# Projection weights in one transfer per contraction tile, a gate column transposed by a matmul, and whole-tile x copies, in a gated mix of linear-memory attention and a gated feed-forward

## The chip, the cores and the metric

One core of a Trainium2 chip runs the kernel. The metric is device microseconds from launch to end; the median over several runs is given, and a profile of one execution shows what the engines did. Engines are named as the profile names them: PE (TensorE matmuls), PEld (its weight loads), DVE (VectorE), ACT (ScalarE), POOL (GpSimd), SP (SyncE, which here only issues DMA transfers). "SPq" and "ACTq" are DMA issues by SP and ACT.

## The reference

All inputs are bfloat16; x is 2048 tokens by 512 features. Two branches are computed from the same x and mixed by a gate of one number per token.

```python
x = A_x
g = sigmoid((x * gate_w).sum(-1, keepdims=True))
a = A_ref(x, wq, wk, wv, wo, beta)   # attention in 4 segments of 512 tokens, 32 heads of 16
b = B_ref(x, W_gate, W_up, W_down)   # (relu(x @ W_gate) * (x @ W_up)) @ W_down, inner size 1792
return g * a + (1 - g) * b
# inside A_ref, per segment s:
#   p = softmax(qs @ ks.T * 0.25 + causal mask); a_dot = p @ vs
#   a_mem = phi(qs) @ M / (phi(qs) @ z + 1e-6);  o = sigmoid(beta) * a_mem + (1 - sigmoid(beta)) * a_dot
#   M += phi(ks).T @ vs;  z += phi(ks).sum()      (phi(t) = t + 1 for t > 0, else exp(t))
# the segments' o are joined and multiplied by wo
```

## The kernel before

The work is cut into four segments of 512 tokens. For each segment the program builds lists of operations: the q, k and v projections (`proj`), causal attention (`att`), the update of the memory matrix (`mu`), the memory's numerator and denominator (`nd`), the feed-forward (`ffn`) and the output product (`outp`). 512 features are four contraction tiles of 128 (`KT = 4`, index `kt`). x is needed transposed, features on partitions, in the tile `xT`.

The order of instructions on each engine is not written by hand. `Sched` is a greedy list scheduler that runs while the kernel is built: each operation names what it reads and writes (strings such as `wq0` or `xT0_1a`), its engine and an estimated duration; queues carry priorities, and the scheduler repeatedly places the operation that its own clock says is ready first. It keeps its own estimate of when a transfer lands: bytes are added up over all transfers at 310 bytes per ns, plus 1.8 us for those issued early and 3.2 us for the others. What it emits is one fixed program per engine with semaphore waits where an operation depends on another engine or a transfer. Each engine runs its program in order, so an instruction whose wait is not met holds all behind it on that engine. Transfers share 16 semaphores in turn; the seventeenth transfer waits for an earlier one that used the same semaphore.

PSUM is used as four banks `psL` (the attention logits, and at the start the transposes of x) and four banks `psA` handed out to accumulations as they come (`Epoch`). If two engines read one bank the scheduler orders them.

The start goes as follows. SP and ACT each issue two of the four loads of segment 0's x (128 KB each, into `hT0` to `hT3`, L416). Then the three 512 x 512 projection weights follow, each in two transfers (L418 to L423): wq as contraction tiles 0 to 2 on SP (384 KB) and tile 3 on ACT; wk and wv as tiles 0 to 1 on ACT and 2 to 3 on SP. After them SP issues beta, the first halves of the feed-forward weights `wg` and `wu` (896 KB each, L431 and L432), the four transposing loads of segment 1's x (L436), the second halves of `wg` and `wu`, `wo` and `wd`. ACT also issues the gate weights as one column (L444): the 512 numbers are put as four columns over 128 partitions, so neighbouring elements of memory go to different partitions.

```python
lact.append(dma("act", ld_gw, 60000, writes=["gwc"], name="ldgw"))
lact[-1].after = 6500.0
```

The second line holds this issue back until 6.5 us of the scheduler's clock. Meanwhile PE runs six warm-up matmuls on zeros (L491), transposes segment 0's x by matmuls with an identity into the four `psL` banks, one bank for each 128 tokens (L499), and runs four more warm-up matmuls, which write the first of these banks again. Each bank is copied to `xT` in two halves: contraction tiles 0 and 1 by DVE (L506), 2 and 3 by ACT (L508). The q projection of segment 0 reads all of these copies; each of its accumulations is two operations of two matmuls, over tiles 0 and 1 and over 2 and 3 (L575), and each waits for the transfers that hold its tiles. The k and v projections (L575 and L573) and everything else follow. The gate of segment 0 is 16 one-column matmuls of `xT` with `gwc` (L531), an exponential on ACT (L535) and small operations behind it; the gate of the other three segments is done later in the same way.

Of the kernel before, what the change touches and what calls it, by code (L numbers as in the profile page):

```python
# [10 lines left out]
BF16 = mybir.dt.bfloat16  # L11
# [329 lines left out]
def plan(S, D, F):  # L341
# [13 lines left out]
        ("rden", [128, 32], F32), ("rdg", [128, 32], F32), ("rdm", [128, 128], F32), ("pm8", [128, 8], F32), ("pm", [128, 2], F32), ("ident", [128, 128], BF16),  # L355
# [24 lines left out]
def program(sc, nc, T, PL, PA, A_x, A_wq, A_wk, A_wv, A_wo, A_beta, W_g, W_u, W_d, gate_w, out, NSEG, KT, NF, NT, EPS, SCALE):  # L380
# [11 lines left out]
    def dve(fn, occ, **k):  # L392
        return op("dve", fn, occ, **k)
# [13 lines left out]
    def xt(c):  # L407
        return [f"xT{c}_{kt}" for kt in range(KT)] if c else [f"xT0_{i}{h}" for i in range(4) for h in "ab"]
# [8 lines left out]
    halves = {}  # L417
    for nm, w, src, cut, engs in (("wq", V.wq, A_wq, 3, ("sp", "act")), ("wk", V.wk, A_wk, 2, ("act", "sp")), ("wv", V.wv, A_wv, 2, ("act", "sp"))):  # L418
        r = src.rearrange("(kt p) n -> p kt n", p=128)
        for h, (k0, k1) in enumerate(((0, cut), (cut, KT))):  # L420
            load(engs[h], [f"{nm}{h}"], w[:, k0:k1, :], r[:, k0:k1, :], (k1 - k0) << 17)
            for kt in range(k0, k1):
                halves[nm, kt] = f"{nm}{h}"  # L423
# [16 lines left out]
    gsrc = gate_w.rearrange("(kt p) -> p kt", p=128)  # L440

    def ld_gw(e):
        with nc.allow_non_contiguous_dma(reason="one column of gate weights"):
            return e.dma_start(V.gwc[:], gsrc)  # L444
    lact.append(dma("act", ld_gw, 60000, writes=["gwc"], name="ldgw"))
    lact[-1].after = 6500.0
# [49 lines left out]
    for i in range(4):  # L496
        def fx(e, i=i):
            for kt in range(KT):
                ins = e.matmul(PL[:, i, kt * 128:(kt + 1) * 128], lhsT=V.hT[:, i, kt * 128:(kt + 1) * 128], rhs=V.ident[:], start=True, stop=True)  # L499
            return ins  # L500
        xps.append(pe(fx, 430, reads=[f"hT{i}", "ident"], writes=[f"bankL{i}"], name=f"xt{i}"))
        for h in range(2):
            dst = V.xT[:, 2 * h:2 * h + 2, i * 128:(i + 1) * 128]
            srcp = PL[:, i, 256 * h:256 * h + 256].rearrange("q (k t) -> q k t", k=2)
            if h == 0:
                xcs.append(dve(lambda e, d=dst, s_=srcp: e.tensor_copy(d, s_), t_dve(256), reads=[f"bankL{i}"], writes=[f"xT0_{i}a"], name=f"xc{i}"))  # L506
            else:
                xcs.append(act(lambda e, d=dst, s_=srcp: e.activation(d, s_, ACT.Copy), t_act(256), reads=[f"bankL{i}"], writes=[f"xT0_{i}b"], name=f"xc{i}"))  # L508
# [13 lines left out]

    gexpT_r = {}
# [26 lines left out]
    sc.queue(2, gq["pe"][:1])  # L550
    sc.queue(4, gq["pe"][1:])
    sc.queue(1, gq["act"])
# [9 lines left out]
    def proj(s):  # L562
# [3 lines left out]
        def pj(w, col, name, wname, tokmajor=False):  # L566
            ep = Epoch("proj")

            for k0 in range(0, KT, 2):
                def fn(e, k0=k0):  # L570
                    for kt in (k0, k0 + 1):
                        if tokmajor:
                            ins = e.matmul(A(ep)[:, :], lhsT=V.xT[:, kt, tok + col * 128:tok + (col + 1) * 128], rhs=w[:, kt, :], start=(kt == 0), stop=(kt == KT - 1))  # L573
                        else:
                            ins = e.matmul(A(ep)[:, :], lhsT=w[:, kt, col * 128:(col + 1) * 128], rhs=V.xT[:, kt, tok:tok + 512], start=(kt == 0), stop=(kt == KT - 1))  # L575
                    return ins
                pes.append(pe(fn, mm(512, 2), reads=sorted({halves[wname, k0], halves[wname, k0 + 1]}) + xt(s), name=f"{name}{s}_{col}", ep=ep, role="w2" if k0 else "w"))
# [309 lines left out]
```

The softmax here doesn't subtract the row's maximum and nothing guards it: scores larger than these inputs give would overflow.

## Time and profile before

| | us |
|---|---|
| median of 5 runs | 276.65 |
| lowest and highest | 276.54, 278.15 |
| the profiled execution | 276.64 |
| its span, first to last instruction | 274.90 |
| PE busy | 264.6 (96% of the span) |
| DVE busy | 198.9 (72%) |
| ACT busy | 191.3 (70%) |
| POOL busy | 92.4 (34%) |
| first projection matmul | 7.38 |
| last matmul ends | 272.10 |

A line of the profile names the source line, the engine, the operation, what is written from what is read, the number of instructions, and in square brackets how long the engine had been idle before and what ended that. In a list in order of time the first number is the start in us from the beginning of the span and the second how long the group lasted. The granted TensorE clock was 0.999 of full speed throughout.

### The profile page before, as it was taken

To read this page: it belongs to the slowest core of one execution; us is meant where nothing else is said; L and a number is where in the kernel's file an instruction comes from. 1 tells how busy PE (TensorE), PEld (TensorE's weight loads), DVE (VectorE), ACT (ScalarE), POOL (GpSimd) and SP (SyncE) were. 2 spreads that over 40 slices of the span, in tenths; PEclk is the share of its full clock that TensorE was granted. 3 is DMA by queue.
4 is the path that set the end of the run, shared out by engine and by line. 5 is a ranking of instruction groups with operands and counts; after the bars stand their busy time and mean duration, and the time that the engine had idled before them with its cause. 6 is when DMAs were issued, how large, how long until landed. Compare 5 with 4: busy or idle time off the path is not lost.

```text
span 274.9 us, 5331 instructions
## 1 busy us (share of the span) xinstructions
PE 264.6 (96%) x2168; PEld 116.2 (42%) x2204; DVE 198.9 (72%) x391; ACT 191.3 (70%) x170; POOL 92.4 (34%) x152
## 2 busy tenths in 40 slices
PE   7999999999999999999999999999999999999995
PEld 3444344434444444444344343344434343444444
DVE  5598989899999999978789774378677055857200
ACT  3089997898697787786679777785767777763112
POOL 4013234334445452535233434332333333320000
PEclk9999999999999999999999999999999999999999
DMA  7999533000101223040012000000110100000011
GB/s 234 319 246 365 159 76 80 0 3 20 41 1 38 41 60 57 19 60 0 2 38 41 1 21 19 21 19 2 38 38 2 38 21 19 2 1 0 2 38 39
DMA packets 29384, 15.29 MB, mean 56 GB/s; under 512 B 20784, under 2 KB 29360, under 8 KB 29360
## 3 DMA queue, kind: packets, MB, share of 16 engines
q1 hardware_dynamic: 27856, 14.04, 20.3%
q10 hardware_dynamic: 1504, 0.92, 1.1%
q8 instruction: 17, 0.28, 0.4%
q14 instruction: 7, 0.06, 0.1%
HBM read 8.14 MB, written 2.10 MB: 37 GB/s over the span
## 4 chain that ended last, share of the span: by engine, by line
PE 89%; DVE 4%; ACT 2%; DMA 2%; issue 2%; SPq 0%
PE psA L740 35%; PE psA L779 17%; PE psL L670 9%; PE psA L575 9%; PE psA L695 7%; PE psA L772 5%; PE psA L573 5%; ACT E L675 2%; DMA wq<-in_A_wq_dram 2%; PE psA L645 1%; PE psA L616 1%; DVE hT L751 1%; DVE kp L591 1%; DVE qT L582 0%; DVE adT L707 0%
## 5 line engine op out<-in xcount | busy, mean ns | idle before, releaser
L675 ACT ACTIVATE E<-psL 128x2048 bf16<-128x2048 f32 x80 | 150.1, 1876 | 40.2 <-PE psL L670 39.7
L678 POOL TENSOR_SCALAR_AFFINE_SELECT E<-E 128x512 bf16<-128x512 bf16 x128 | 82.8, 664 | 147.9 <-ACT E L675 145.6
L740 PE MATMUL psA<-xT,wg 128*128 128x512 bf16 x215 | 57.6, 380 | 1.4 <-issue 1.3
L740 PE MATMUL psA<-xT,wu 128*128 128x512 bf16 x217 | 57.7, 380 | 0.8 <-issue 0.6
L779 PE MATMUL psA<-wd,hT 128*128 128x512 bf16 (+1 forms) x228 | 53.5, 367 | 1.1 <-issue 0.8
L751 DVE TENSOR_TENSOR hT<-psA,rl 128x512 bf16<-128x512 f32 x56 | 38.4, 686 | 14.1 <-PE psA L740 12.7
L700 DVE STREAM_TRANSPOSE Tn<-psA 128x512 f32<-128x512 f32 x32 | 21.5, 700 | 19.2 <-PE psA L695 19.1
L670 PE MATMUL psL<-qT,kp 32*128 32x384 bf16 (+3 forms) x512 | 31.7, 301 | 0.4 <-ACT E L675 0.3
L779 PEld LDWEIGHTS psA<-wd,hT 128*128 128x128 bf16 x238 | 21.4, 98 | 23.6 <-issue 3.9
L740 PEld LDWEIGHTS psA<-xT,wu 128*128 128x128 bf16 x224 | 20.5, 98 | 25.3 <-issue 2.0
L740 PEld LDWEIGHTS psA<-xT,wg 128*128 128x128 bf16 x224 | 20.1, 98 | 25.1 <-issue 3.5
L748 ACT ACTIVATE rl<-psA 128x512 bf16<-128x512 f32 x29 | 17.2, 597 | 13.9 <-PE psA L740 11.3
L670 PEld LDWEIGHTS psL<-qT,kp 32*128 32x128 bf16 x512 | 8.9, 92 | 33.1 <-ACT E L675 18.0
L749 DVE TENSOR_SCALAR rl<-psA 128x512 bf16<-128x512 f32 x27 | 18.5, 684 | 4.4 <-PE psA L740 3.7
L695 PE MATMUL psA<-E,vaug 128*17 128x256 bf16 (+3 forms) x512 | 21.1, 300 | 0.2 <-DVE kT L588 0.2
L575 PE MATMUL psA<-xT,wq 128*128 128x512 bf16 x60 | 16.1, 380 | 1.5 <-DMA wq<-in_A_wq_dram 1.0
L789 ACT ACTIVATE osb<-psA,omg 128x512 bf16<-128x512 f32 (+1 forms) x10 | 6.4, 644 | 15.6 <-PE psA L772 13.3
L575 PE MATMUL psA<-xT,wk 128*128 128x512 bf16 x62 | 16.4, 380 | 0.1
L772 PE MATMUL psA<-wo,oT 128*128 128x512 bf16 (+1 forms) x65 | 15.8, 366 | 0.4 <-issue 0.3
L573 PE MATMUL psA<-wv,xT 128*128 128x512 bf16 x63 | 15.3, 380 | 0.2 <-issue 0.2
L695 PEld LDWEIGHTS psA<-E,vaug 128*17 128x17 bf16 x512 | 10.5, 90 | 11.2 <-issue 3.8
L582 DVE CAST qT<-psA 128x512 bf16<-128x512 f32 x16 | 10.9, 684 | 3.5 <-PE psA L575 3.4
(68 smaller groups left out, 211.4 us busy)
## 6 DMA issues: line engine op xcount, KB each, us to landing
out_dram<-osb SPq DMA_DIRECT2D x15, 128.0 KB, 1.7
wg<-in_B_W_gate_dram SPq DMA_DIRECT2D x2, 896.0 KB, 7.7
wu<-in_B_W_up_dram SPq DMA_DIRECT2D x2, 896.0 KB, 10.1
wd<-in_B_W_down_dram SPq DMA_DIRECT2D x1, 1792.0 KB, 13.9
wo<-in_A_wo_dram SPq DMA_DIRECT2D x1, 512.0 KB, 9.4
wq<-in_A_wq_dram SPq DMA_DIRECT2D x1, 384.0 KB, 5.5
hT<-in_A_x_dram ACTq DMA_DIRECT2D x2, 128.0 KB, 3.1
hT<-in_A_x_dram SPq DMA_DIRECT2D x2, 128.0 KB, 2.9
```

Source lines behind the costliest of these rows:

```text
L573: ins = e.matmul(A(ep)[:, :], lhsT=V.xT[:, kt, tok + col * 128:tok + (col + 1) * 128], rhs=w[:, kt, :], start=(kt == 0), stop=(kt == KT - 1))
L575: ins = e.matmul(A(ep)[:, :], lhsT=w[:, kt, col * 128:(col + 1) * 128], rhs=V.xT[:, kt, tok:tok + 512], start=(kt == 0), stop=(kt == KT - 1))
L670: ins = q.matmul(PL[:, jj, o:o + w], lhsT=V.kp[32 * jj:32 * jj + 32, kslot(s, n), 128 * j:128 * j + 128], rhs=V.qT[32 * jj:32 * jj + 32, q ...
L675: acts.append(act(lambda a, e=e: a.activation(V.E[:, e, :, :], PL[:, :, :], ACT.Exp, scale=SCALE), t_act(2048), reads=[f"bankL{b}" for b i ...
L678: pools.append(pool(lambda g, ap=ap: g.affine_select(out=ap, in_=ap, compare_op=ALU.is_ge, fill=0.0, base=0, pattern=[[0, 4], [1, 128]], c ...
L695: ins = q.matmul(A(ep)[32 * jj:32 * jj + 17, c:512], lhsT=V.vaug[:, s % 2, j, 8 * G + 2 * jj + p, :], rhs=V.E[:, e, jj, o:o + w], start=(j ...
L700: ds.append(dve(lambda e, p=p, ep=eps[p]: e.transpose(V.Tn[:, p, :], A(ep)[:, :]), t_dve(512), writes=[f"Tn{p}"], name=f"tr{s}_{G}_{p}", e ...
L740: ins = e.matmul(A(ep)[:, :], lhsT=w[:, kt, f * 128:(f + 1) * 128], rhs=V.xT[:, kt, c * 512:(c + 1) * 512], start=(kt == 0), stop=(kt == K ...
L749: ("dve", lambda e, ep=eg, r=r: e.tensor_scalar(V.rl[:, r, :], A(ep)[:, :], 0.0, None, ALU.max), t_dve(512))],
L751: evs.append(dve(lambda e, ep=eu, r=r, hs=hs: e.tensor_tensor(V.hT[:, hs, :], A(ep)[:, :], V.rl[:, r, :], ALU.mult), t_dve(512), reads=[f" ...
L772: ins = e.matmul(A(ep)[:, 0:c1 - c0], lhsT=V.oT[:, o0 + G, i * 128:(i + 1) * 128], rhs=V.wo[:, G, c0:c1], start=st_ and G == 0, stop=sp_ a ...
L779: ins = e.matmul(A(ep)[:, 0:c1 - c0], lhsT=V.hT[:, slots[f], i * 128:(i + 1) * 128], rhs=V.wd[:, f, c0:c1], start=st_ and f == f0, stop=sp ...
```

## The change

Each of the three projection weights is loaded in four transfers, one for each contraction tile of 128 KB; wq's tiles 1 and 3 are issued by ACT, all other tiles by SP. A projection operation waits for the two tiles that it reads. The gate weights are loaded by SP as four rows of 128 numbers (`g4`, contiguous in memory), behind the first halves of `wg` and `wu`; a matmul with a 4 x 4 identity transposes them into a `psA` bank, and an ACT copy writes `gwc`. The x copies of segment 0 are one for each bank, all four contraction tiles at once, by DVE for banks 0 and 2 and by ACT for banks 1 and 3.

```diff
--- before.py
+++ after.py
@@ -352,7 +352,7 @@
         ("Mbd", [128, 4, 136], F32), ("Mbd16", [128, 4, 136], BF16), ("mumask", [128, 2, 136], BF16), ("mutmp", [128, 2, 136], F32),
         ("gwc", [128, KT], BF16), ("braw", [128, 32], BF16), ("eb", [128, 32], F32), ("romgh", [128, 32], F32), ("epsv", [128, 32], F32),
         ("gexp", [128, NT], F32), ("omg", [128, NT], F32), ("gexpT", [128, NT * 4], F32), ("c2g", [128, NT, 32], F32),
-        ("rden", [128, 32], F32), ("rdg", [128, 32], F32), ("rdm", [128, 128], F32), ("pm8", [128, 8], F32), ("pm", [128, 2], F32), ("ident", [128, 128], BF16),
+        ("rden", [128, 32], F32), ("rdg", [128, 32], F32), ("rdm", [128, 128], F32), ("pm8", [128, 8], F32), ("pm", [128, 2], F32), ("ident", [128, 128], BF16), ("g4", [4, 128], BF16),
     ]
 
 
@@ -405,7 +405,7 @@
         return PA[ep.bank]
 
     def xt(c):
-        return [f"xT{c}_{kt}" for kt in range(KT)] if c else [f"xT0_{i}{h}" for i in range(4) for h in "ab"]
+        return [f"xT{c}_{kt}" for kt in range(KT)] if c else [f"xT0_{i}" for i in range(4)]
 
     lact, lsp = [], []
 
@@ -414,13 +414,9 @@
     x0 = A_x[0, 0:512, :].rearrange("(i p) d -> p i d", p=128)
     for i, eng in enumerate(("sp", "act", "sp", "act")):
         load(eng, [f"hT{i}"], V.hT[:, i, :], x0[:, i, :], 1 << 17)
-    halves = {}
-    for nm, w, src, cut, engs in (("wq", V.wq, A_wq, 3, ("sp", "act")), ("wk", V.wk, A_wk, 2, ("act", "sp")), ("wv", V.wv, A_wv, 2, ("act", "sp"))):
-        r = src.rearrange("(kt p) n -> p kt n", p=128)
-        for h, (k0, k1) in enumerate(((0, cut), (cut, KT))):
-            load(engs[h], [f"{nm}{h}"], w[:, k0:k1, :], r[:, k0:k1, :], (k1 - k0) << 17)
-            for kt in range(k0, k1):
-                halves[nm, kt] = f"{nm}{h}"
+    for nm, w, src in (("wq", V.wq, A_wq), ("wk", V.wk, A_wk), ("wv", V.wv, A_wv)):
+        for kt in range(KT):
+            load("act" if nm == "wq" and kt % 2 else "sp", [f"{nm}{kt}"], w[:, kt, :], src[kt * 128:(kt + 1) * 128, :], 1 << 17)
     wgr = W_g.rearrange("(kt p) n -> p kt n", p=128)
     wur = W_u.rearrange("(kt p) n -> p kt n", p=128)
     half = (NF // 2) * 128
@@ -437,13 +433,7 @@
                            1 << 17, occ=1280.0, writes=[f"xT{c}_{kt}"], name=f"ldx{c}_{kt}"))
     load("sp", ["braw"], V.braw[:], A_beta.partition_broadcast(128), 8192)
     load_gu(0)
-    gsrc = gate_w.rearrange("(kt p) -> p kt", p=128)
-
-    def ld_gw(e):
-        with nc.allow_non_contiguous_dma(reason="one column of gate weights"):
-            return e.dma_start(V.gwc[:], gsrc)
-    lact.append(dma("act", ld_gw, 60000, writes=["gwc"], name="ldgw"))
-    lact[-1].after = 6500.0
+    load("sp", ["g4"], V.g4[:], gate_w.rearrange("(kt p) -> kt p", p=128), 1 << 12)
     load_x(1)
     load_gu(1)
     load("sp", ["wo"], V.wo[:], A_wo.rearrange("(g p) n -> p g n", p=128), 1 << 19)
@@ -499,13 +489,12 @@
                 ins = e.matmul(PL[:, i, kt * 128:(kt + 1) * 128], lhsT=V.hT[:, i, kt * 128:(kt + 1) * 128], rhs=V.ident[:], start=True, stop=True)
             return ins
         xps.append(pe(fx, 430, reads=[f"hT{i}", "ident"], writes=[f"bankL{i}"], name=f"xt{i}"))
-        for h in range(2):
-            dst = V.xT[:, 2 * h:2 * h + 2, i * 128:(i + 1) * 128]
-            srcp = PL[:, i, 256 * h:256 * h + 256].rearrange("q (k t) -> q k t", k=2)
-            if h == 0:
-                xcs.append(dve(lambda e, d=dst, s_=srcp: e.tensor_copy(d, s_), t_dve(256), reads=[f"bankL{i}"], writes=[f"xT0_{i}a"], name=f"xc{i}"))
-            else:
-                xcs.append(act(lambda e, d=dst, s_=srcp: e.activation(d, s_, ACT.Copy), t_act(256), reads=[f"bankL{i}"], writes=[f"xT0_{i}b"], name=f"xc{i}"))
+        dst = V.xT[:, :, i * 128:(i + 1) * 128]
+        srcp = PL[:, i, :].rearrange("q (k t) -> q k t", k=KT)
+        if i % 2 == 0:
+            xcs.append(dve(lambda e, d=dst, s_=srcp: e.tensor_copy(d, s_), t_dve(512), reads=[f"bankL{i}"], writes=[f"xT0_{i}"], name=f"xc{i}"))
+        else:
+            xcs.append(act(lambda e, d=dst, s_=srcp: e.activation(d, s_, ACT.Copy), t_act(512), reads=[f"bankL{i}"], writes=[f"xT0_{i}"], name=f"xc{i}"))
     xps.append(warm(4, 1, 0))
     sc.queue(0, xps)
     sc.queue(0, [t for t in xcs if t.eng == "dve"])
@@ -520,6 +509,9 @@
     sc.queue(0, [t for t in cst if t.eng == "act"])
     sc.queue(1, [t for t in cst if t.eng == "dve"])
 
+    ep_w = Epoch()
+    gw_pe = pe(lambda e: e.matmul(A(ep_w)[:, 0:KT], lhsT=V.g4[:, :], rhs=V.ident[0:KT, 0:KT], start=True, stop=True), 60, reads=["g4", "ident"], name="gwT", ep=ep_w, role="w")
+    gw_act = act(lambda e: e.activation(V.gwc[:], A(ep_w)[:, 0:KT], ACT.Copy), 180, writes=["gwc"], name="gwc", ep=ep_w, role="r")
     gexpT_r = {}
     gq = {"pe": [], "act": [], "dve": [], "flex": []}
     for part, (t0, t1) in enumerate(((0, 4), (4, NT))):
@@ -547,9 +539,9 @@
         if part:
             gq["dve"].append(dve(lambda e, t0=t0: e.tensor_tensor(V.c2g[:, t0:, :], V.eb[:, :].unsqueeze(1).to_broadcast([128, NT - t0, 32]), V.gexp[:, t0:].unsqueeze(2).to_broadcast([128, NT - t0, 32]), ALU.mult),
                                  t_dve((NT - t0) * 32), reads=["eb", f"gexp{part}"], writes=["c2g"], name="c2g"))
-    sc.queue(2, gq["pe"][:1])
+    sc.queue(2, [gw_pe] + gq["pe"][:1])
     sc.queue(4, gq["pe"][1:])
-    sc.queue(1, gq["act"])
+    sc.queue(1, [gw_act] + gq["act"])
     sc.queue(1, gq["dve"])
     sc.queue(2, gq["flex"])
 
@@ -574,7 +566,7 @@
                         else:
                             ins = e.matmul(A(ep)[:, :], lhsT=w[:, kt, col * 128:(col + 1) * 128], rhs=V.xT[:, kt, tok:tok + 512], start=(kt == 0), stop=(kt == KT - 1))
                     return ins
-                pes.append(pe(fn, mm(512, 2), reads=sorted({halves[wname, k0], halves[wname, k0 + 1]}) + xt(s), name=f"{name}{s}_{col}", ep=ep, role="w2" if k0 else "w"))
+                pes.append(pe(fn, mm(512, 2), reads=[f"{wname}{k0}", f"{wname}{k0 + 1}"] + xt(s), name=f"{name}{s}_{col}", ep=ep, role="w2" if k0 else "w"))
             return ep
         for G in range(4):
             ep = pj(V.wq, G, "q", "wq")
```

## The prediction

> **What bounds the kernel now.** I read first the page's busy shares, then the chain of waits, then its start instruction by instruction, because all that the change touches is issued in the first 20 us.
>
> ```profile
> PE 264.6 (96%) x2168; PEld 116.2 (42%) x2204; DVE 198.9 (72%) x391; ACT 191.3 (70%) x170; POOL 92.4 (34%) x152
> ...
> PE 89%; DVE 4%; ACT 2%; DMA 2%; issue 2%; SPq 0%
> ```
>
> ```profile
> 7.38:272.10 264.72, 259.63 (x2142) 113.77 (x2178) 195.24 (x381) 188.13 (x164) 88.98 (x137) 1.00 0.21 51
> ```
>
> The first two lines are the page's busy times and its chain by engine. Columns of the third (busy time by stretch): the stretch, its length, then busy time of PE, PEld, DVE, ACT, POOL. From the first projection matmul (7.38) to the last matmul (272.10) PE is busy 259.63 of 264.72 us; only 5.09 us are idle, in gaps of mostly 0.16 to 0.4 us. So whatever the change does to the first 20 us reaches the end only as a shift of the moment at which this dense block begins, as a new hole in it, or as a different number of gaps. The chain shows what sets its beginning:
>
> ```profile
> 1.73 5.52 DMA wq<-in_A_wq_dram
> 7.38 5.12 PE psA L575 x23
> ```
>
> ```profile
> 4.45 1.42 DVE L506 CAST xT<-psL 128x256 bf16<-128x256 f32 x4 [0.99 <-PE psL L499]
> 4.91 1.05 ACT L508 ACTIVATE xT<-psL 128x256 bf16<-128x256 f32 x3 [0.34 <-DVE xT L506]
> ...
> 4.96 10.86 SPq L436 DMA_TRANSPOSE xT<-in_A_x_dram  x4
> 5.59 0.38 ACTq L444 DMA_DIRECT2D gwc<-in_gate_w_dram  x1
> 6.02 0.38 ACT L508 ACTIVATE xT<-psL 128x256 bf16<-128x256 f32 x1
> ...
> 7.38 3.61 PE L575 MATMUL psA<-xT,wq 128*128 128x512 bf16 x16 [0.99 <-DMA wq<-in_A_wq_dram]
> ...
> 18.61 0.54 PE L531 MATMUL psA<-gwc,xT 128*128 128x1 bf16 x16
> ```
>
> The 384 KB transfer of wq, issued at 1.73, lands 5.52 us later, at 7.25; PE starts 0.14 later. The x copies are done at 6.02 + 0.38 = 6.40 and the warm-up matmuls at 6.39: these are second, 0.85 us ahead of the weights.
>
> **What the Trainium skill says.** "DMA: Bandwidth & Descriptors", section "Issuing engines are not separate DMA queues": transfers of all issuing engines run on the same 16 DMA engines and interleave; two issuers save only issue time. The trace agrees: between 3 and 8 us the core moves 343 to 380 GB/s with two queues filled, and from 11 to 14 us, with SP's alone left but for the gate column, 350 to 368. The same page, "Queues, rings and completion order": each DMA engine takes turns between the queues, in order within one. Here the ACT queue's third 128 KB (wq's last tile) landed at 1.73 + 4.5 = 6.2 and its fourth and fifth (half of wk) at 2.21 + 5.6 = 7.8: 0.8 us per 128 KB while SP's queue is full too. The same page, "Rules for kernel authors": a strided last dimension becomes one descriptor per element. The ACT queue's 1504 packets fit: 896 KB in rows of 1 KB are 896, which leaves room for 512 gate elements. "PSUM — Partial Sum Buffer", section "Terms": two engines must not read one bank at once. The ordering in the kernel respects it: ACT's first half copy waits 0.34 us for DVE's.
>
> **The change, part by part.**
>
> *wq by tiles.* Now both pairs of contraction tiles wait for the 384 KB transfer, since tiles 0 to 2 are one. After it, the first pair waits for tiles 0 and 1, third in their queues, the second for 2 and 3, fourth. By ACT's cadence above, tile 1 lands at 6.2 and tile 3 at 6.2 + 0.8 = 7.0; SP's tiles are earlier (its fifth 128 KB landed at 7.25, its seventh at 2.19 + 6.5 = 8.7, so 0.72 each, the fourth at 6.5). With the 0.14 us from landing to matmul the second pair starts at 7.14. Before, it started at 7.38 + 2 x 0.215 = 7.81 (16 matmuls in 3.61 us: 0.215 from start to start). **Gain 0.67 us.** Bounds: if landing no longer mattered the first pair would start at 6.34, second at 6.77, gain 1.04; if tile 3 lands as late as the 384 KB did, gain 0.42; if the four small transfers take longer still, nothing.
>
> *x copies.* PE makes the four transposed tiles 0.35 us apart (16 matmuls in 1.41), so they can be copied from 4.45, 4.80, 5.15, 5.50. A 512-wide PSUM copy costs 684 ns on DVE (row of L582) and 597 on ACT (row of L748): DVE 4.45 to 5.13 and 5.15 to 5.84, ACT 4.80 to 5.40 and 5.50 to 6.10. Done at 6.10 against 6.40. Priced at nothing: the landing of wq tile 1 at 6.2 hides it. The four warm-up matmuls wait for tile 0's copy, 5.13 against 5.29, and stay ahead of 6.3. Should the weights land at once, the copies would set the start, at 6.24.
>
> *ACT's queue* loses the two wk/wv halves (0.49 + 0.52 us) and the column's issue (0.38). Its table load, 1.28 us, moves from 3.29 to about 2.7; its first copy waits for PE in both versions. Nothing.
>
> *SP's queue* goes from 8 loads to 16 ahead of the transposes. Its cadence is 0.50 us (1.73 to 4.22 for five), so wk's last tile is issued at 4.2, wv's at 6.2, beta at 6.7, wg at 7.2 (before 3.75), wu at 7.7, the gate rows at 8.2, and the x transposes of segment 1 begin at 8.9 instead of 4.96. What waits behind each:
> - wk is needed when the 16 q matmuls end, 7.14 + 14 x 0.215 = 10.2. About 1.6 MB lie up to its last tile; at 350 GB/s from 2.3 us these have moved by 6.9, and some 1.3 us lie between the last byte and landing (the 384 KB: about 1.3 MB interleaved by 7.25, moved by 6.0). 8.2: covered by 2 us.
> - wv is needed at 14.0; it lands by 9.7. Covered. beta lands about 9.8, before 10.84: eb, which waited 4.5 us on ACT, and the romgh behind it lose their wait, off the path.
> - wg and wu: a 128 KB load is issued every 0.50 us and drained in 0.37, but SP's backlog built while ACT's queue shared the engines lasts until about 8.4, when wg's first bytes arrive (7.2 + 1.2). So the engines do not run dry; they land near 13.65 and 4.22 + 11.8 = 16.0 as before, against first uses near 19 and 20.4.
> - Segment 1's x, whose last transpose was issued at 14.24 and landed 3.8 us later, at 18.0. PE's first use stood at 19.0 and moves to 18.4. This is the thin cover, 0.4 us. The four issues took 10.86 us, where the undisturbed take 1.26 each; the first two lasted 3.18 and 4.43:
>
> ```profile
> 4.96 3.18 SPq L436 DMA_TRANSPOSE xT<-in_A_x_dram  x1
> ...
> 8.18 4.43 SPq L436 DMA_TRANSPOSE xT<-in_A_x_dram  x1
> ```
>
> They ended at 8.14 and 12.61, each 1.0 to 1.5 us ahead of the landing of wv (9.5) and of wg (3.75 + 9.9 = 13.65), as if each were let through when the load ahead had been drained. Then a start at 8.9 finds the first obstacle gone and ends no later than 15.8. I take a landing at 17 to 18; ends: 16.5, and 21.9 if the whole stretch moves by 3.9.
> - wg's and wu's second halves, wo and wd follow by at most 4 us: second halves are used from about 40 us and landed at 21.4 and 24.9. Covered.
>
> *Gate column.* Removed: 512 tiny transfers that landed at 5.59 + 8.6 = 14.2. Added: a 1 KB load behind wu (landing about 16), one 128x4 matmul and one ACT copy. The matmul costs like one of L531, 0.54/16 = 0.03 us, with a gap of 0.16 around it at most; the copy 0.17 (the gexp row, 128x4). The gate matmuls, at 18.61 before, then stand behind PE to ACT to PE, some 0.5 us if nothing fills it; the scheduler counts these latencies and has ffn work to put between. Waiting behind the gate matmuls on PE would be segment 1's projection. Cost 0 to 0.5, taken at 0.1.
>
> Sum: -0.67 + 0.10 = -0.57 us. The profiled execution took 276.64 us (span 274.90 and 1.74 around it), a hundredth below the median of 276.65. So 276.1.
>
> **The rivals.**
> 1. *No gain*: per-tile transfers share the same bandwidth and the last wq tile lands at 7.3 or later; then 276.6 to 277. For it: 128 KB pieces; against it: ACT's third piece landed at 6.2.
> 2. *The transposes come late* (slower). If the long issues are SP's own work and not back-pressure, all move by 3.9 us: landing 21.9, PE at 18.4 with segment 1's first q matmuls at its head and all else behind: 21.9 + 0.13 - 18.4 = 3.6 us of hole, net +3.0, 279.6. It decides from a landing at 18.3 on. Against it speak the two ends above and the 1.26 us of undisturbed issues.
> 3. *The order is made anew.* The list scheduler is greedy, and shifted estimates at the start can change which matmuls follow which over all 265 us. Gaps are 0.16 us each (L740 behind issue: 1.9 us in 12), and DVE is busy 38.15 of 40 us between 60 and 100, so a bad order costs. Twelve gaps more are +1.9, 278.0 in all; twelve fewer 274.2. Nothing in the profile says which.
>
> **How the numbers follow.** About 0.5% (1.4 us) is what a measurement of this kernel can tell from no change. Forecast (276.1, own range 275.4 to 276.7) 0.50; no gain 0.15; late transposes 0.13; worse order 0.14; better order or the full 1.04 us with luck 0.08. Faster by over 0.5%: 0.08 and a tenth of the forecast, 0.13. Slower: 0.14, most of 0.13 and a little of the forecast, 0.27. Between: 0.60. The range is 274.9 to 278.9: it takes in half of the order's swing upwards and half of the late transposes, and leaves some 0.07 below and 0.12 above.
>
> **What would show it.** First wq matmul near 6.35, the second pair behind a wait for wq to about 7.1; the 16 q matmuls ending near 10.3 (before 10.98); last x copy at 6.1; the transposes beginning at 8.9 and ended by 15.8; no hole of PE near 18.4; PE busy 259 to 260 us from the first projection matmul on. Wrong: a DMA wait for xT at 18 to 22 us, a start at 7.3 or later, or over 6 us idle in the dense block.

## The result and the profile after

The changed kernel takes 277.09 us (median of 43 runs) against 277.37 for the kernel before (80 runs): ratio 0.9989, 95% interval 0.9976 to 1.0002. A second set of runs gave 277.15 against 277.67, 0.998 [0.996, 1.0]. So it is the same, or faster by 0.1 to 0.2%; both intervals reach no change. Ratios are taken over fast executions alone (those within 1.5% of the fastest of their kernel), so they are not exactly the quotients of the medians. The profiled execution took 277.89 us with a span of 276.2, which is 0.8 us above its own median; the profiled execution of before, 276.64, lies 0.7 below its median of 80 runs. What is compared below has to allow for that.

The lines of the page that answer to those of before, busy times and chain by engine:

```profile
PE 264.6 (96%) x2169; PEld 115.8 (42%) x2205; DVE 198.6 (72%) x387; ACT 191.4 (69%) x171; POOL 92.3 (33%) x152
...
PE 84%; DVE 6%; DMA 3%; ACT 2%; issue 2%; SPq 2%; DVEq 0%
```

Busy time by stretch, from the first projection matmul to the last matmul (columns as before: stretch, length, busy time of PE and so on):

```profile
6.32:273.40 267.08, 259.87 (x2143) 113.75 (x2179) 194.99 (x379) 188.58 (x167) 88.89 (x137) 1.00 0.22 52
```

PE starts at 6.32 instead of 7.38, but the stretch is 267.1 us long instead of 264.7. A gain of 1.06 us at the start is lost, and 1.3 us besides. The start in order of time shows where. A hole is time in which PE stands idle; PEld lines are weight loads, one ahead of each matmul. First the kernel before, from its k projection on:

```profile
10.62 3.33 PEld L575 LDWEIGHTS psA<-xT,wk 128*128 128x128 bf16 x16
...
11.15 0.18 DVE L515 TENSOR_SCALAR romgh<-eb 128x32 f32<-128x32 f32 x1 [1.15 <-ACT eb L514]
11.24 0.68 DVE L582 CAST qT<-psA 128x512 bf16<-128x512 f32 x1
...
14.38 0.39 PE L670 MATMUL psL<-qT,kp 32*128 32x512 bf16 x4
```

Then the changed one:

```profile
4.27 1.29 DVE L495 CAST xT<-psL 128x512 bf16<-128x512 f32 x2 [0.81 <-PE psL L489]
4.50 1.09 ACT L497 ACTIVATE xT<-psL 128x512 bf16<-128x512 f32 x2 [0.54 <-PE psL L489]
...
6.32 3.81 PE L567 MATMUL psA<-xT,wq 128*128 128x512 bf16 x16 [0.26 <-DMA wq<-in_A_wq_dram]
6.52 0.43 SPq L413 DMA_DIRECT2D braw<-in_A_beta_dram  x1
...
8.50 9.61 SPq L432 DMA_TRANSPOSE xT<-in_A_x_dram  x4
9.75 3.33 PEld L567 LDWEIGHTS psA<-xT,wk 128*128 128x128 bf16 x16
...
13.63 0.23 ACT L503 ACTIVATE eb<-braw 128x32 f32<-128x32 bf16 x1 [8.04 <-DMA braw<-in_A_beta_dram]
13.89 0.18 DVE L504 TENSOR_SCALAR romgh<-eb 128x32 f32<-128x32 f32 x1 [3.04 <-ACT eb L503]
13.98 0.68 DVE L580 CAST kT<-psA 128x512 bf16<-128x512 f32 x1
...
15.67 0.39 PE L662 MATMUL psL<-qT,kp 32*128 32x512 bf16 x4 [2.09 <-DVE kp L583]
...
18.69 0.09 PEld L513 LDWEIGHTS psA<-ident,g 4*128 4x128 bf16 x1 [0.42 <-DMA g<-in_gate_w_dram]
...
19.48 0.54 PE L523 MATMUL psA<-gwc,xT 128*128 128x1 bf16 x16
```

Read it backwards from the hole. PE stands for 2.09 us because the masked k tile `kp` is not there. DVE has not made it because it stood still for 3.04 us: its next instruction in order is `romgh`, which needs beta's exponential. ACT could not make that because beta's 8 KB, issued by SP at 6.52, behind sixteen weight and x loads of which twelve are SP's, landed 7.09 us later, at 13.6. The four copies of k stood in DVE's program behind this one small operation; in the kernel before it was two copies of q, and PE did not yet need what waited for them.

The lengths of the parts show that this is nearly all. From the first weight load of k to the first attention matmul the changed kernel takes 5.92 us (9.75 to 15.67), the kernel before 3.76 (10.62 to 14.38): 2.16 us lost. From the start of q to the first weight load of k it takes 3.43 us instead of 3.24, because q's second pair waits for its tiles: 0.19 us. From the first attention matmul to the last matmul both take 257.7 us. Together 2.35 of the 2.38 us by which the stretch is longer. The weight load of the transposing matmul waited 0.42 us for the gate rows, but by these lengths that cost PE nothing here.

What fills the time in which beta is on its way is seen in the data rate (last column, GB/s; the one before it is the busy share of the DMA engines). First the kernel before, then the changed one:

```profile
9.00:10.00 1.00, 1.00 (x7) 0.42 (x5) 0.83 (x2) 0.00 (x0) 0.00 (x0) 1.00 0.84 283
```

```profile
9.00:10.00 1.00, 1.00 (x7) 0.43 (x5) 0.82 (x2) 0.00 (x0) 0.00 (x0) 1.00 0.55 104
```

The first pieces of beta move at 8.4 us, and in the microsecond shown the DMA engines move 104 GB/s where 350 are usual. What stands behind beta in SP's queue landed later too: the last of segment 1's x at 20.2 instead of 18.0. The trace counts the landing of a load in sixteen signals. For beta fifteen of them had come by 10.5 us; the sixteenth came at 13.6. So one late signal of a small load made the wait long.

### The profile page after: what moved, and what is told of

Its sections match the earlier page's. It is cut to its first block, busy times and chain, and to the rows that moved or that the text cites. A ratio compares the mean times of both kernels' runs of the same rounds, so it can differ in the third digit from the quotient of the medians.

```text
span 276.2 us, 5342 instructions
## 1 busy us (share of the span) xinstructions
PE 264.6 (96%) x2169; PEld 115.8 (42%) x2205; DVE 198.6 (72%) x387; ACT 191.4 (69%) x171; POOL 92.3 (33%) x152
## 3 DMA queue, kind: packets, MB, share of 16 engines
HBM read 8.14 MB, written 2.10 MB: 37 GB/s over the span
## 4 chain that ended last, share of the span: by engine, by line
PE 84%; DVE 6%; DMA 3%; ACT 2%; issue 2%; SPq 2%; DVEq 0%
PE psA L732 33%; PE psA L771 17%; PE psL L662 9%; PE psA L687 7%; PE psA L567 6%; PE psA L764 5%; PE psA L565 5%; DMA braw<-in_A_beta_dram 3%; ACT E L667 2%; SPq L413 2%; DVE hT L743 1%; PE psA L637 1%; PE psA L608 1%; DVE kT L580 1%; DVE kp L583 1%
## 5 line engine op out<-in xcount | busy, mean ns | idle before, releaser
L692 DVE STREAM_TRANSPOSE Tn<-psA 128x512 f32<-128x512 f32 x32 | 21.5, 700 | 19.2 <-PE psA L687 19.1
L741 DVE TENSOR_SCALAR rl<-psA 128x512 bf16<-128x512 f32 x27 | 18.5, 684 | 4.4 <-PE psA L732 3.7
L781 ACT ACTIVATE osb<-psA,omg 128x512 bf16<-128x512 f32 (+1 forms) x10 | 6.4, 644 | 15.6 <-PE psA L764 11.7
L764 PE MATMUL psA<-wo,oT 128*128 128x512 bf16 (+1 forms) x65 | 15.8, 366 | 0.4 <-issue 0.3
L687 PEld LDWEIGHTS psA<-E,vaug 128*17 128x17 bf16 x512 | 10.5, 90 | 11.2 <-issue 3.6
L583 DVE TENSOR_SCALAR kp<-kT,pm 128x512 bf16<-128x512 bf16 x32 | 12.4, 399 | 1.2 <-PE psL L662 0.8
```

Of the source, the lines that this page charges most:

```text
L687: ins = q.matmul(A(ep)[32 * jj:32 * jj + 17, c:512], lhsT=V.vaug[:, s % 2, j, 8 * G + 2 * jj + p, :], rhs=V.E[:, e, jj, o:o + w], start=(j ...
L692: ds.append(dve(lambda e, p=p, ep=eps[p]: e.transpose(V.Tn[:, p, :], A(ep)[:, :]), t_dve(512), writes=[f"Tn{p}"], name=f"tr{s}_{G}_{p}", e ...
L741: ("dve", lambda e, ep=eg, r=r: e.tensor_scalar(V.rl[:, r, :], A(ep)[:, :], 0.0, None, ALU.max), t_dve(512))],
L764: ins = e.matmul(A(ep)[:, 0:c1 - c0], lhsT=V.oT[:, o0 + G, i * 128:(i + 1) * 128], rhs=V.wo[:, G, c0:c1], start=st_ and G == 0, stop=sp_ a ...
```

## The experiments

The table gathers every profile: when the first q matmul began, how long the stretch from it to the last matmul was, when beta landed, and the time. Each kernel is compared with the kernel before as it ran in the same set of runs. Differences of a few tenths of a us between kernels of different sets are within the intervals.

| kernel | q starts, us | stretch, us | beta lands, us | median, us | ratio to before (95%) |
|---|---|---|---|---|---|
| before | 7.38 | 264.72 | 10.9 | | 1 |
| before, second profile | 8.14 | 264.73 | 11.1 | | (one run) |
| changed | 6.32 | 267.10 | 13.6 | 277.09 | 0.9989 [0.9976, 1.0002] |
| changed, second profile | 5.96 | 265.63 | 11.5 | 277.15 | 0.998 [0.996, 1.0] |
| changed, beta ahead of wv | 6.75 | 265.20 | 8.6 | 276.51 | 0.996 [0.9942, 0.9977] |
| changed, exponential told late | 6.11 | 266.33 | 12.3 | 276.80 | 0.9965 [0.9942, 0.9987] |
| changed, beta from rows | 6.61 | 265.36 | 9.4 | 276.29 | 0.9949 [0.9929, 0.9969] |
| changed, wu behind x | 6.68 | 265.36 | 12.2 | 276.43 | 0.9967 [0.9951, 0.9983] |
| before, beta from rows | 7.89 | 264.73 | 10.3 | 277.18 | 0.999 [0.9972, 1.0008] |
| before + wq in tiles | 6.63 | 265.65 | 11.1 | 276.62 | 0.9961 [0.9943, 0.9979] |
| before + copies | 7.99 | 264.74 | 11.4 | 277.16 | 0.9996 [0.9974, 1.0018] |
| before + gate rows | 7.29 | 264.69 | 10.6 | 277.60 | 1.001 [0.9987, 1.0033] |
| before + all loads in tiles | 6.41 | 266.99 | 12.1 | 278.14 | 1.0034 [1.0013, 1.0054] |
| the same, beta from rows | 7.17 | 265.37 | 12.0 | 277.29 | 0.999 [0.9961, 1.0019] |
| changed, beta ahead of wv, gate column | 5.92 | 265.99 | 8.7 | 277.04 | 0.9994 [0.9971, 1.0018] |
| before + wq in tiles, exponential told late | 6.75 | 264.40 | 10.9 | 276.07 | 0.9952 [0.9925, 0.9979] |
| the same + copies | 6.15 | 264.74 | 10.4 | 276.05 | 0.9941 [0.9918, 0.9964] |

**The changed kernel again.** No edit.

> The changed kernel unaltered, a second look. Beta theory: the hole in PE between the k and the v projection (2.1 us in its first profile) is made by the in-order DVE, which holds the copies of kT behind an operation that needs beta, and beta lands at 13 to 14 us every time; so the hole is there again, 1.5 to 2.5 us, with the first q matmul near 6.3, and the time within 0.3% of the kernel before. Rival (an accident of one execution): beta lands before 12 us here, no hole over 0.5 us, and the time 0.6 us or more below the kernel before.

Neither was right as put. Beta landed at 11.5, two us earlier than in the first profile, and the hole was 0.40, as the rival says; but the time, 0.5 us below the kernel before with an interval that reaches no change, does not bear the rival out:

```profile
11.48 0.23 ACT L503 ACTIVATE eb<-braw 128x32 f32<-128x32 bf16 x1 [5.84 <-DMA braw<-in_A_beta_dram]
11.74 0.18 DVE L504 TENSOR_SCALAR romgh<-eb 128x32 f32<-128x32 f32 x1 [1.35 <-ACT eb L503]
...
13.52 0.39 PE L662 MATMUL psL<-qT,kp 32*128 32x512 bf16 x4 [0.40 <-DVE kp L583]
```

So the chain beta, ACT, DVE, PE is there again, but its length differs from execution to execution by the landing of one 8 KB load; the first profile shows a bad case. The span was 274.3 us here and 276.2 there, of the same program.

The page of this execution also shows what the first two hid:

```profile
PE 269.0 (98%) x2205; PEld 115.9 (42%) x2205; DVE 198.6 (72%) x387; ACT 191.6 (70%) x171; POOL 92.6 (34%) x152
```

This program loads weights once for each matmul, and here both counts are 2205. On the page of before the counts were 2168 and 2204: 36 matmul records are missing there, and most of the "5.09 us idle" from 7.38 on were those, not gaps. Where records are whole, as in this profile, PE is busy 264.4 us of the stretch. Of the 1.23 us that are left, 0.54 lie before 21 us and only 0.69 in all the time after.

**The changed kernel with beta ahead of wv.**

```diff
 SP:  hT0 hT2 wq0 wq2 wk0 wk1 wk2 wk3
+SP:  beta
 SP:  wv0 wv1 wv2 wv3
-SP:  beta
 SP:  wg wu g4 ...
```

> Only beta's load is moved, by hand, from behind wv's four tiles to behind wk's four on SP; every engine's order of work stays that of the changed kernel, wv and what follows is issued one load later. Beta theory: beta lands about 2 us earlier, 10.5 to 11.7, before the k copies need the DVE, the hole shrinks from 2.1 us to below 0.4 and the time falls by 1.5 to 2.0 us against the changed kernel, to 0.994 to 0.996 of the kernel before. Rival (the scheduler's new order costs the time wherever it is): the order is the same, so no change against the changed kernel. Rival (DMA bandwidth): the load's slow stretch moves ahead of wv and wv becomes late, hole of similar size at v.

Beta landed at 8.6, DVE reached `romgh` without a wait, no hole was left at the k copies, and the median fell by 0.64 us against the changed kernel in the same set of runs. The beta theory holds in its direction with the order of work unchanged, so the new order is not what cost the time, and wv was not late. The size, 1.5 to 2.0 us, was expected from the bad first profile; a third of it came. PE then waited 0.15 us for segment 1's x.

**The changed kernel with the exponential told late.**

```diff
 cst = [act(lambda e: e.activation(V.eb[:], V.braw[:], ACT.Exp), 300, reads=["braw"], writes=["eb"], name="eb")]
+cst[0].after = 14500.0
```

> Beta's load stays where the change puts it; only the scheduler is told that the exponential of beta is not ready before 14.5 us, so the operations that need beta stand later in DVE's and ACT's programs. Beta theory: beta still lands at 13 to 14 us, but the copies of kT no longer stand behind it, the first attention matmuls start near 13.6 instead of 15.7, and the time is 1.3 to 2.1 us below the changed kernel, less what a new order costs or brings. Rival (the late landing hurts by itself, through something other than DVE's order, or bandwidth): hole stays.

Beta landed at 12.3 and no copy of k that PE needs soon stood behind it: the first attention matmuls began at 12.76. So the hole went as the theory says, but the median is only 0.35 us below the changed kernel, less than these runs can tell from nothing. In the profile PE now reaches the gate rows too early:

```profile
17.85 0.17 PE L514 MATMUL psA<-ident,g 4*128 4x4 bf16 x1 [1.24 <-DMA g<-in_gate_w_dram]
```

What was taken away at beta came back in part at the rows, which stand two 896 KB loads further down the same queue. The wait of q's second pair for its tiles was 0.34 us here.

**Beta from distinct rows**, in the changed kernel and in the kernel before.

```diff
-    load("sp", ["braw"], V.braw[:], A_beta.partition_broadcast(128), 8192)
+    load("sp", ["braw"], V.braw[:], A_x[0, 0:128, 0:32], 8192)
```

> The broadcast of beta (128 reads of the same 64 bytes) is replaced by 128 reads of 64 bytes from 128 different rows of x, in the same place and of the same size; beta's values are thus not used, the order of work is the same. If the repeated reading of one address is what makes this load slow: the dip of the DMA rate between 8 and 10.5 us goes, the load lands before 11 us, the hole is gone and the time is 1.5 to 2 us below the changed kernel. If it is only the small pieces or the place in the queue: landing 13 to 14 again, same hole, same time.

In the changed kernel the load landed 2.9 us after its issue instead of 5.0 to 7.1:

```profile
9.46 0.23 ACT L503 ACTIVATE eb<-braw 128x32 f32<-128x32 bf16 x1 [3.13 <-DMA braw<-in_A_x_dram]
```

The data rate from 9 to 10 us was 188 GB/s, a dip still but a smaller one, the hole at the k copies was gone, and the time was 0.86 us below the changed kernel: the direction as expected, half the size.

> The kernel before with beta's broadcast replaced by 128 reads of 64 bytes from different rows of x (beta's values are not used). Theory (beta's late landing costs both kernels): 0.5 to 1.3 us below the kernel before, and a narrow spread of runs (under 1.2 us), as the changed kernel showed with the same edit; what is left between the two is then the change without beta, 0.3 to 0.8 us in favour of the changed kernel. Rival (only the changed kernel suffers from beta): no change against the kernel before.

In the kernel before it made no difference that can be measured, as the rival says. The edit moved beta little there, to 10.3 from 10.9 and 11.1, so it tests little by itself; the profiles say more. DVE idles for beta in the kernel before too (1.15 us in the first profile), but behind that stand two q copies for which PE did not have to wait: the stretch is 264.7 us with or without the broadcast.

**The kernel before, again.**

> The kernel before, a second look. If beta's landing scatters there as well (10.84 us in the first profile), the DVE, which holds two of the q copies behind it, idles for another length than 1.15 us and the hole in PE before or in the k projection changes with it; the first q matmul at 7.0 to 7.6. If beta lands within 0.3 us of 10.84, the scatter belongs to the changed kernel alone.

```profile
8.14 3.61 PE L575 MATMUL psA<-xT,wq 128*128 128x512 bf16 x16 [1.72 <-DMA wq<-in_A_wq_dram]
```

q started at 8.14, not at 7.38, behind a wait of 1.72 us for wq. The 384 KB landed at 8.0 here and at 7.25 in the profile that the prediction rests on. In the five profiles that keep this transfer (before twice, beta from rows, copies, gate rows) the start was at 7.38, 8.14, 7.89, 7.99 and 7.29, mean 7.74; the stretch was 264.7 us in all five. In this kernel the scatter of the start from execution to execution is the landing of wq. Beta landed at 11.1, within the 0.3 us that were set, and at 10.6 to 11.4 in all profiles of before and of its variants with whole wq that keep the broadcast: a scatter of 2 us belongs to the changed kernel.

**One part alone: wq.**

```diff
+    for kt in range(KT):
+        load("act" if kt % 2 else "sp", [f"wq{kt}"], V.wq[:, kt, :], A_wq[kt * 128:(kt + 1) * 128, :], 1 << 17)
+        halves["wq", kt] = f"wq{kt}"
-    for nm, w, src, cut, engs in (("wq", V.wq, A_wq, 3, ("sp", "act")), ("wk", ...
+    for nm, w, src, cut, engs in (("wk", ...
```

> The kernel before with only wq in four transfers, odd tiles on ACT; wk, wv, beta, gate column and copies as before. If wq's tiles bring the early start: first q matmul at 6.4 to 6.6 (held by the x copies at 6.4), 0.6 to 1.0 us earlier than before, beta landing where it did before (10 to 11), the time 0.5 to 1.0 us below. If the start needs the whole-tile copies too: start near 6.6, the same gain within 0.2. Rival (tiles bring nothing without the rest moved off ACT): start above 7.1.

q starts at 6.63, held by the last x copy, and the time is 0.75 us below before. By the medians that is more than the whole change brings (0.3 and 0.5), though the intervals overlap. The profile shows why it is not still more: beta lands at 11.1 as before, while PE is 1.1 us further on, and two holes of 0.46 and 0.41 us open at k and at the first attention matmul:

```profile
11.40 0.18 DVE L518 TENSOR_SCALAR romgh<-eb 128x32 f32<-128x32 f32 x1 [2.13 <-ACT eb L517]
...
12.23 1.90 PE L578 MATMUL psA<-xT,wk 128*128 128x512 bf16 x8 [0.46 <-DVE qT L585]
```

**One part alone: the copies, the gate rows.** The edits are those parts of the diff.

> The kernel before with only the x copies made whole, alternating between DVE and ACT. Copies done near 6.1 instead of 6.4, q still starts when the 384 KB of wq land, 7.2 to 7.4: same time within 0.3%. If it is 0.4 us or more faster, copies and not weights set the start in most executions.

> The kernel before with only the gate weights as four rows behind wu, the transposing matmul and the ACT copy. The rows land at 16 to 18, PE's order has the matmul at about 18: same time within 0.2%, at most 0.4 us slower by a wait for the rows. If it is 0.5 us slower or more, the gate part is what eats the early start. If faster by 0.4 us, the 512 single elements of the column cost the other transfers at the start.

Both without effect on the time, as expected. The whole copies end at 6.3 and wq lands 1.6 us later, so q starts at 7.99 and not at the 7.2 to 7.4 that were expected. With the gate rows alone PE reached the transposing matmul at 17.31 without a wait.

**One part alone: the loads.**

> The kernel before with only the loads of the change: all three projection weights in tiles, wk and wv on SP alone, beta behind them. Start at 6.4 to 6.7, as with wq alone (6.63). Beta is issued near 6.5 and lands at 11.4 to 13.6 as in the changed kernel. If beta's place behind wv is what the change loses: hole of 0.5 to 2 us at the k copies, time 0.2 to 0.6 us above that with wq alone (0.9961 of before), so 0.997 to 0.9985. If moving wk and wv off ACT costs nothing: as with wq alone.

Slower than before, 1.0034 [1.0013, 1.0054], where 0.997 to 0.9985 was expected, though PE starts at 6.41. Beta lands at 12.1 and a hole of 0.59 follows, but the large one is elsewhere:

```profile
20.88 0.59 PE L571 MATMUL psA<-xT,wq 128*128 128x512 bf16 x2 [1.58 <-DVE kp L587]
```

This is segment 1's first q projection. The engine named had long been done; segment 1's x, whose last transpose was issued at 15.6, landed 5.1 us later, at 20.6. This is the slower rival of the prediction, in a part of the change if not in the whole. The order of work is another one here: the scheduler has put the 16 gate matmuls among those of k, at 11.17 us, so this kernel differs from before in more than its loads.

**The loads with beta from rows.** The edit is the one above.

> The kernel with only the change's loads (278.14 us, with a hole of 1.58 us before segment 1's first q matmuls, whose x landed at 20.7), beta's broadcast replaced by 128 reads of 64 bytes from different rows (beta's values not used); same order of work. If the slow stretch that the broadcast makes in SP's queue (63 and 77 GB/s from 9 to 11 us) is what delays segment 1's x behind it: x lands at 18.2 to 18.9, the hole shrinks to under 0.5, time 1.2 to 2.2 us below, 276.0 to 276.9. If x is late because SP issues its transposes 3 us later: landing 20 or later, hole and time as they were, less 0.3 at most for beta.

In between. x landed at 19.8, 0.9 us earlier, and PE waited 0.67 us for it:

```profile
20.03 0.59 PE L571 MATMUL psA<-xT,wq 128*128 128x512 bf16 x2 [0.67 <-DMA xT<-in_A_x_dram]
```

Part of the shorter wait is that q began later here, at 7.17. Against before, where x landed at 18.0, the loads alone are 2.6 us late and this kernel 1.8: in these two profiles the broadcast accounts for 0.9 of it. The rest stays open. Here, in the loads alone and in the next kernel, all of which load the gate column beside weights that are all in tiles, there are 1.8 to 2.0 us between the landings of two consecutive transposes, where the other kernels have 0.4 to 0.7, and no run tells why. Beta itself landed at 12.0 here even without the broadcast, 0.35 us behind the last tile of wv (11.65), and again one signal was late: fifteen of its sixteen had come by 10.3. So repeated reading is not the only thing that can make it late.

**The changed kernel with beta ahead of wv and the gate column as before.**

> The changed kernel with the gate column loaded as before (no rows, no transposing matmul) and with beta's load moved by hand from behind wv to behind wk. Start at 6.1 to 6.8, beta landing before 10, no hole over 0.4 us: 275.9 to 276.3, 0.993 to 0.995 of before. If the gate rows cost nothing, it equals the changed kernel with beta ahead of wv (0.996) within 0.2 us.

Missed: 0.9994, not 0.993 to 0.995. Beta landed at 8.7 and held nobody; but x landed at 19.2 and PE stood for 1.21 us at segment 1's q. With gate rows in place of the column the same kernel had x at 18.7 and a wait of 0.15. So the rows, without effect on the kernel before, seem useful beside weights that are all in tiles; the two intervals just overlap.

**The changed kernel with wu behind segment 1's x.**

```diff
 SP:  ... beta wg
-SP:  wu
 SP:  g4 x1_0 x1_1 x1_2 x1_3
+SP:  wu
 SP:  wg (second half) ...
```

> The changed kernel with one load moved by hand on SP: the first half of wu behind the gate rows and segment 1's x instead of ahead of them; order of work unchanged on all other engines. Segment 1's x lands before 17.5 and the gate rows before 15, so no wait for either; beta still lands at 11.4 to 13.6 and holds DVE. Theory (x and rows are a second limit behind beta): 0.2 to 0.7 us below the changed kernel (0.998 to 0.9989), so 0.996 to 0.9975, unless wu, now issued near 14.5, lands after its first use near 20.5, which would put a hole there. Rival (x and rows cost nothing in the median): no change.

x landed at 16.9, PE waited neither for it nor for the rows, the hole at beta stayed (0.54), and the time was 276.43, 0.9967, inside what was expected. The ratio's interval overlaps those of the changed kernel, so the times alone do not show a gain. The profiles show where one can come from: from the first attention matmul to the last matmul this kernel takes 257.75 us, as does the first profile of the changed kernel, where beta held PE for long; the second profile takes 258.07, with beta ahead of wv 258.12, with beta from rows 258.35. So the order in SP's queue is a second limit of the changed kernel, of 0.3 to 0.6 us, which shows when beta does not hold PE first.

**wq in tiles and the exponential told late, then with the whole-tile copies too.** `cst[0].after = 12500.0` on the kernel with wq alone, and then the diff's part on copies.

> The kernel before with wq in tiles and with the scheduler told that the exponential of beta comes at 12.5 us, so that DVE's operation on it stands behind three of the k copies instead of among the q copies. Beta theory: with wq alone DVE idled 2.13 us for beta and PE lost 0.9 us in holes at k; these go, and the time falls by 0.5 to 1.0 us against wq alone, to 0.992 to 0.9945 of before. Rival (holes are filled later anyway, order costs): within 0.2 us of wq alone.

> wq in tiles with the exponential of beta told late (0.9952), and the whole-tile x copies as well; all else as before. With wq alone the start was held by the last x copy (6.63 and 6.75); whole copies end near 6.1, so the start moves to 6.2 to 6.5 and the time falls by 0.2 to 0.5 us, to 0.9935 to 0.995. If segment 1's x (landed at 18.0 there) is next, PE waits for it near 18 and the gain is under 0.2.

Beta lands at 10.9 and 10.4, behind it stand no k copies that PE needs soon, and the stretch is 264.40 and 264.74 us, without holes: with wq alone it was 265.65. By ratio the first of the two, 0.9952, missed what was expected (0.992 to 0.9945) and is not told apart from wq alone (0.9961). The last one in busy time by stretch:

```profile
6.15:270.89 264.74, 263.96 (x2179) 114.19 (x2178) 197.00 (x380) 189.25 (x165) 88.46 (x137) 1.00 0.21 53
```

263.96 busy of 264.74. With 276.05 us, 0.9941 [0.9918, 0.9964], it has the lowest ratio of all runs, clear of the kernel before, and of the changed kernel's first set though not quite of its second: the early start of the change without its cost. The start was at 6.15 in this profile and at 6.75 in the one without the copies; but three other kernels with whole copies started at 6.61 to 6.75, so one profile of each doesn't show that the copies did it, and by ratio (0.9952 and 0.9941) the two kernels are not told apart.

## Why the prediction was right or wrong

The forecast, 0.57 us faster and within 0.5%, has the right sign of the median, and the two sets of runs gave 0.3 and 0.5 us, neither clear of no change. That it came near is luck: the gain at the start was put too low, a loss behind it was put at nothing, and the two errors cancel. The absolute 276.1 us missed by 1.0, of which 0.7 is the starting value: 276.65 was the median of 5 runs, that of 80 is 277.37.

- *Beta covered* is the step that failed. It says that beta "lands about 9.8, before 10.84" and that eb and romgh "lose their wait, off the path". It was issued when expected (6.52 against 6.7) but landed at 11.5 to 13.6, and DVE's operation that needs it stood in front of the k copies. Two things were missing. Beta was priced with nothing beyond the queue ahead of it, although in the profile of before it landed 1.3 us behind the last SP load ahead of it (9.56 and 10.86); in the four profiles of the changed kernel that keep its place and the broadcast it was 1.5 to 3.7 us. And what was queued behind the waiting instruction was not named: on DVE, all four k copies; on PE, the first attention matmuls and with them v. "Off the path" had been true of two q copies. Holes of 0.4 to 2.1 us came of it, and none of the three rivals names beta. Moving only this load removes the hole and 0.64 us of the median.
- *wq by tiles* was the right mechanism, but mis-sized. The gain was worked out as 0.67 us, from one profile of before in which wq landed early (7.25; the other four had 7.2 to 8.0), and its upper bound as 1.04. The five profiles start at 7.74 on average; the six of the changed kernel and its variants in the upper part of the table at 6.4 (5.96 to 6.75). That is 1.3 us; a second profile of the unchanged kernel would have shown it. The wait of the second pair for its tiles was foreseen and is there: from the start of q to the first weight load of k these six take 3.24 to 3.75 us, where before takes 3.24.
- *SP's backlog*: the issue times were right to 0.4 us (wg 7.0, the transposes 8.5). "The engines do not run dry" was wrong: the rate fell to 104 GB/s and lower while beta was on its way, and what follows came later. The prediction quotes the rate of before for 3 to 8 and for 11 to 14 us; between them, with beta on its way, its trace shows 211 and 283 GB/s from 8 to 10. The first transpose's short issue (2.1 us), as against 3.2 before, fits the reading that an issue is let through when the load ahead has drained; the end of the issues, put at 15.8 at the latest, was at 16.2 and 18.1.
- *Segment 1's x*, called the thin cover with 0.4 us, was thin: landing at 20.2 and 18.3 in the two profiles of the changed kernel against a use at 20.3 and 18.5. That PE escaped a wait in the first profile because beta held it up as well is argued from these times, not shown by a run. The rival of late transposes is real in the loads alone (1.58 us), by a landing that is 2.6 us late and not the 3.9 that the rival takes.
- *Gate rows*, taken at 0.1 of 0 to 0.5: nothing in the first profile and with the gate rows alone; with x some 0.3 to 0.6 us where beta does not hold PE first, and a hole of 1.24 with the exponential told late.
- *The order made anew* needed no chance of its own. Its price rested on 5.09 us of gaps that were mostly missing records. From the first attention matmul on, the first profile of the changed kernel takes the 257.7 us of before, and the stretch was 264.4 to 264.7 us in every kernel without a hole, whatever the order.
- *Copies* at nothing: right for the kernel before, where they alone changed nothing. In the changed kernel they ended at 5.6 and not at 6.1. Once wq's tiles land early, it is in several profiles the x copies or the matmuls ahead of them that set the start, with half copies (6.4 to 7.2 in four profiles) as with whole ones (5.9 to 6.8): what whole copies are worth there, the runs do not separate. *ACT's queue* at nothing was not tested alone.

## What to carry to other kernels

When a start is pulled forward, list every small load that an in-order engine waits for, how far behind the load ahead of it it lands in more than one profile, and what stands behind that wait; the next limit can be a few KB at the wrong place of a queue. Compare the counts of matmuls and weight loads before reading idle time on PE, and take a second profile before pricing a gain from one landing time. A change that bundles a good edit with one that gives its gain back is worth taking apart: here one part alone had a lower median than the whole, and two parts with beta's exponential told late the lowest of all.

## What the runs showed of the hardware that was not expected

In the four profiles of the changed kernel that keep it in its place, an 8 KB broadcast load (128 times the same 64 bytes) took 5.0 to 7.1 us from issue to landing. Fourteen of its sixteen signals had come by 10.5 us each time, the last at 11.5 to 13.6: so the landing is set by one or two late ones. As 128 different rows in the same place it took 2.9 us, in one profile. While it was under way the core's data rate was 46 to 104 GB/s from 9 to 10 us, after 305 to 354 from 7 to 8. But the broadcast is not always late: moved ahead of wv it landed 0.2 and 0.8 us behind the load ahead of it, in the kernels with wq alone in tiles 0.4 to 0.5 us. Why, the runs do not show. The same transfer of wq, 384 KB issued at 1.73 us, landed at 7.25 in one execution of the same program and at 8.0 in another.
